# PV of a head group in one run, reciprocals shared by head groups, pruned waits, and scores issued only once ready: a change to a fused adaLN transformer block

## The chip, the cores and the metric

The kernel runs on one core of a Trainium2 chip. The metric is the device time of one execution in microseconds (us); medians of several executions are given. A ratio of two kernels is the mean time of one kernel's fast runs over that of the other's fast runs of the same rounds, so it is not quite the ratio of the medians that stand beside it.

Short names: PE is TensorE's matmuls, PEld its weight loads, ACT ScalarE, DVE VectorE, POOL GpSimd, SP the queue that issues DMAs. L712 is line 712 of the kernel in question, so the same statement has different line numbers before and after (scores: L712 before, L700 after).

## The reference, cut to what matters

```python
# S = 2048 tokens, D = 1024, 32 heads of 32, ONE key/value head, F = 3584; bf16 in and out
mod = silu(c) @ w_mod                      # six vectors: sa, ca, ga, sb, cb, gb
h = layernorm(x) * (1 + ca) + sa
q = (h @ wq) as 32 heads;  k = h @ wk;  v = h @ wv
p = softmax(q @ k.T / sqrt(32));  o = p @ v
x = x + ga * (o @ wo)
h = layernorm(x) * (1 + cb) + sb
x = x + gb * ((silu(h @ w1) * (h @ w3)) @ w2)
```

## The kernel before

The queries are cut into 8 blocks of 256. In a block, 8 *head groups* of 4 heads follow one another, and in a head group 8 *steps* of 2 key tiles. A step is 8 score matmuls (S: 32 rows of the array each, four side by side), then two exps of 128x1024 from PSUM into one of the U buffers. PV matmuls (V: 32 columns each, four side by side) read U. VectorE adds the U buffers of four steps into a TR buffer, and matmuls with a matrix of ones (D) sum TR over the keys, which gives the softmax denominators. After a block's attention come the output projection, layernorm, transposes and the feed-forward of that block ("post"). These use the full array (F) and are slotted into the attention of the next block.

Nothing of this is ordered by hand. Each operation is a node with an assumed duration, and a list scheduler in the kernel fixes the order of every engine when the kernel is built. The parts that the change touches:

```python
slack = 0.12 if e in ("pe", "act") else 0.02      # us
...                                               # scores have the first rank on PE
pick = min((c for c in cands if c[0] <= t + (slack if c[1].prio <= 1 else 0.001)), key=key)
```

`t` is the earliest time at which any candidate can start on the engine. Scores that can start at most 0.12 us later than `t` win against feed-forward work that could start at `t`: PE is parked for them.

```python
NU = 10; VB = 8; R = 8; NTR = 5     # U buffers; key tiles per PV run; TR buffers
...
if len(pend) < vb:                  # vb = 4 steps = 8 key tiles
    continue
g = batch(pend, qn)                 # a PV run into a PSUM bank of its own; reads the key "ATTD"
...                                 # first run: copy the bank to ASB; second run: add it to ASB
for h in range(qn // 128):          # per head group: 2 reciprocals of 128x128
    G.add("dve", lambda e, h=h: e.reciprocal(DSB[:, ...], DSB[:, ...]), ...)
G.add("dve", ... QT[:, f] = ASB * DSB, writes=qkeys(f, q0, qn) + ["ATTD"], ...)
```

Of the eight PSUM banks, six hold scores during attention. The other two are shared by PV/D and by all feed-forward work. Key "ATTD" makes the next head group's PV wait for the normalised output of this one.

The softmax here doesn't subtract the row's maximum and nothing guards it: scores larger than these inputs give would overflow.

Of the kernel before, what the change touches and what calls it, by code (L numbers as in the profile page):

```python
# [3 lines left out]
BF16 = mybir.dt.bfloat16  # L4
F32 = mybir.dt.float32
# [3 lines left out]
P = 128  # L9
# [4 lines left out]
class Node:  # L14
    __slots__ = ("eng", "fn", "dur", "lat", "deps", "prio", "seq", "mode", "acq", "touch",
                 "start", "vis", "pos", "ndeps", "users", "need_inc", "cnt", "dsem", "dval", "nbytes", "est", "cls",
                 "sbanks", "after")
# [8 lines left out]
class Dag:  # L26
# [76 lines left out]
    def schedule(self, banks):  # L103
# [41 lines left out]
        while left:  # L145
# [30 lines left out]
            slack = 0.12 if e in ("pe", "act") else 0.02  # L176
# [70 lines left out]
    def emit(self, tail):  # L247
# [3 lines left out]
        for e in ENGS:  # L251
            seen = {}
            dseen = {}
            for n in self.order[e]:
                need = {}
                dneed = {}
                for d in n.deps:
                    if d.dsem is not None:
                        k = id(d.dsem)
                        if dseen.get(k, 0) < d.dval and (k not in dneed or dneed[k].dval < d.dval):  # L260
                            dneed[k] = d
                    elif d.eng == e == "pe":
                        continue
                    elif seen.get(d.eng, -1) < d.pos and (d.eng not in need or need[d.eng].pos < d.pos):
                        need[d.eng] = d
                for k, d in need.items():
                    seen[k] = d.pos
                    d.need_inc = True
                for k, d in dneed.items():
                    dseen[k] = d.dval  # L270
                waits[id(n)] = (list(need.values()), list(dneed.values()))
# [55 lines left out]
def build(nc, x_in, wq_in, wk_in, wv_in, wo_in, w1_in, w3_in, w2_in, c_in, wmod_in, out, S, D, F):  # L327
# [11 lines left out]
    NU = 10  # L339
    VB = 8  # L340
    R = 8
    NTR = 5
# [20 lines left out]
    ASB = sb("ASB", [P, QB], F32)  # L363
    DSB = sb("DSB", [P, QB], F32)
    WKR = sb("WKR", [P, NC, 4, 32], BF16)
    SCT = sb("SCT", [P, NC], BF16)
# [5 lines left out]
    ONES = sb("ONES", [P, 32], BF16)  # L372
# [36 lines left out]
    def grp():  # L409
        return Group()  # L410


    G.add("pool", lambda e: e.memset(ONES[:], 1.0), writes=["ONES"], dur=0.1)
# [247 lines left out]
    def vmms(e, g, part, last, npk, qn):  # L661
        for n, (pu, pk) in part:
            for j, kt in enumerate(pk):
                for gg in range(4):
                    r = e.matmul(PB[g.bank][32 * gg:32 * gg + 32, 0:qn], V[:, kt, :],  # L665
                                 U[:, pu, (gg * npk + j) * qn:(gg * npk + j + 1) * qn], start=n == 0 and j == 0,
                                 stop=n == last and j == len(pk) - 1, tile_position=(0, 32 * gg),
                                 skip_group_check=True)
        return r

    def batch(pend, qn):

        g = grp()
        last = len(pend) - 1
        npk = 512 // qn
        for w0 in range(0, len(pend), 2):
            part = tuple(enumerate(pend))[w0:w0 + 2]
            dep = pend if w0 == 0 else pend[w0:w0 + 2]
            G.add("pe", lambda e, part=part: vmms(e, g, part, last, npk, qn),
                  reads=sorted({("V", kt // 4) for _, pk in dep for kt in pk}) + ["ATTD"] +  # L680
                  [k for pu, _ in dep for k in (("U", pu, 0), ("U", pu, 1), ("UR", pu))],
                  dur=len(pend[w0:w0 + 2]) * (npk * qn / 2400 + 0.007), lat=0.2, cls="V", mode="V",
                  acq=g if w0 == 0 else None, groups=[(g, "w")])
        return g

    def attention(q0, qn):
# [4 lines left out]
        per_t = ns // (R // npk)  # L691
        per_t = R // npk
        vb = VB // npk
        for f in range(NC):
            pend = []
            trs = []
            for s in range(ns):
# [46 lines left out]
                if len(pend) < vb:  # L744
                    continue
                g = batch(pend, qn)
                pend = []
                if s < ns - 1:
                    if s == vb - 1:
                        G.add("dve", lambda e, g=g: e.tensor_copy(ASB[:, 0:qn], PB[g.bank][:, 0:qn]),  # L750
                              writes=["ASB"], groups=[(g, "r")], dur=dve_t(qn), prio=1)
                    else:
                        G.add("dve", lambda e, g=g: e.tensor_tensor(ASB[:, 0:qn], ASB[:, 0:qn], PB[g.bank][:, 0:qn],
                                                                    ALU.add),
                              reads=["ASB"], writes=["ASB"], groups=[(g, "r")], dur=dve_t(qn), prio=1)
                    continue

                def dmm(e, g=g, trs=tuple(trs)):
                    nn = len(trs) * npk
                    for x in range(nn):  # L760
                        tr, j = trs[x // npk], x % npk
                        for gg in range(4):
                            r = e.matmul(PB[g.bank][32 * gg:32 * gg + 32, qn:2 * qn], ONES[:],  # L763
                                         TR[:, tr, (gg * npk + j) * qn:(gg * npk + j + 1) * qn], start=False,
                                         stop=x == nn - 1, tile_position=(0, 32 * gg), skip_group_check=True)
                    return r
# [183 lines left out]
```

## Time and profile before

| | before |
|---|---|
| time, median | 1261.6 us (1261.06 to 1262.0) |
| PE, DVE, ACT busy | 92%, 82%, 80% of the span |
| last exp ends at | 1066 us |
| streaming of all matmuls at 2.4 GHz | 958 us |

The page of the kernel before, engines (busy us, share of the span, instructions), the granted clock of TensorE in tenths over 40 slices, and the chain that ended last:

```profile
PE 1161.1 (92%) x15762; PEld 760.2 (60%) x15809; DVE 1026.9 (82%) x1475; ACT 1011.3 (80%) x1146; POOL 32.0 (3%) x51
...
PEclk9897999999999999998999899998999989999999
...
ACT 46%; PE 31%; issue 10%; DVE 9%; DMA 3%; SPq 1%; POOL 1%; DVEq 0%; ACTq 0%
```

The chain names ACT first. That is misleading here, and the windows view of the same kernel shows why. Its columns are the stretch, its length, then busy time (and instructions) of PE, PEld, DVE, ACT, POOL, then granted clock, DMA share, GB/s:

```profile
900.00:1000.00 100.00, 97.19 (x1394) 61.87 (x1398) 85.63 (x115) 100.00 (x114) 1.68 (x2) 1.00 0.62 175
1000.00:1100.00 100.00, 94.47 (x1251) 71.53 (x1245) 74.58 (x111) 62.32 (x72) 0.79 (x2) 0.97 0.64 176
1100.00:1180.00 80.00, 78.80 (x700) 67.63 (x700) 40.50 (x68) 8.81 (x14) 1.58 (x4) 1.00 1.05 282
1180.00:1259.00 79.00, 74.18 (x680) 66.25 (x677) 34.57 (x52) 8.81 (x14) 0.00 (x0) 1.00 0.97 246
```

ACT is full until 1000 us and almost idle in the last 159 us, in which PE goes on at 94% and more. That is feed-forward work for which PE found no time earlier. Every us that PE wins during attention shortens this tail.

The waits view of the kernel before (engine, line, releaser: us in all, times, longest), and three lines of its groups of VectorE instructions (busy us, mean ns, idle before):

```profile
PEld SP L712 <- ACT UREG L722: 166.5, 453, 1.7
PE SP L712 <- ACT UREG L722: 26.5, 46, 1.4
```

```profile
L774 DVE RECIPROCAL DSB<-DSB 128x128 f32<-128x128 f32 x128 | 119.4, 939 | 0.4
L750 DVE COPY ASB<-PB 128x256 f32<-128x256 f32 x64 | 26.7, 418 | 6.1 <-PE PB L665 6.0
L769 DVE TENSOR_TENSOR ASB<-ASB,PB 128x256 f32<-128x256 f32 x63 | 26.2, 416 | 25.4 <-PE PB L763 25.1
```

Weight loads before scores wait for ScalarE 453 times, 0.37 us on average. The timeline of PE before, in mid-attention (start, us, operation, count), shows the rhythm: scores (L712) every 1.8 us, feed-forward (L869) between, one of the two PV runs (L665) and the denominators (L763):

```profile
645.14 1.48 PE L869 MATMUL PB<-WREG,HREG 128*128 128x256 bf16 x12
646.56 0.40 PE L712 MATMUL SP<-QT,KT 32*128 32x256 bf16 x8
646.89 0.83 PE L869 MATMUL PB<-WREG,HREG 128*128 128x256 bf16 x6
647.64 1.06 PE L665 MATMUL PB<-UREG,V 128*32 128x256 bf16 x32
648.63 0.40 PE L712 MATMUL SP<-QT,KT 32*128 32x256 bf16 x8
648.96 0.62 PE L763 MATMUL PB<-UREG,ONES 128*32 128x256 bf16 x16
649.51 0.94 PE L869 MATMUL PB<-WREG,HREG 128*128 128x256 bf16 x7
```

Busy time of PE hides gaps here, because a matmul's modelled end lies after the start of the next one (645.14 + 1.48 us is later than 646.56). The Trainium skill also warns that matmul busy time is no good measure of how close a kernel is to the peak ("Perfetto Trace Analysis", Identifying the Most-Contended Engine); the account below agrees, with some 950 us of streaming in 1161 us of busy time. So I also sum **start times**: the gap between two successive matmuls (or sets of four side by side) is the difference of their starts, less columns / 2.4 GHz. Six F matmuls of 256 columns start at 646.89 and take 6 x 0.107 = 0.64 us; PV starts at 647.64, so 0.11 us went into the change. The smallest usual gap is 0.096 to 0.108 us for a change of array shape (F to S 0.098, S to F 0.102, V to S or F 0.108). Within one kind it is 0.003 us (F), 0.013 us (S) and 0.005 us (V, D). I call these floors and everything above them a *stall*.

### The profile page before, as it was taken

Reading aid. Unit: us, or ns where it says so; the run is one execution under the profiler, and the core shown is the slowest. Engines: PE = TensorE matmul, PEld = TensorE weight load, DVE = VectorE, ACT = ScalarE, POOL = GpSimd, SP = SyncE. Lnnn points to the kernel's source line nnn. Section 1 sums busy time; section 2 is a strip of 40 time slices with the busy share of each in tenths; the row PEclk is TensorE's granted clock in tenths of the full one; section 3 lists DMA queues with packets and bytes.
Section 4 is the critical chain, followed back from the end, with each engine's and each line's share of the span. In section 5 each row is a group of like instructions: output and inputs, shape, how many; then the busy total and the mean of one; then the engine's idle time right before and its main releaser. Section 6 shows DMA issues by size and latency. Waiting matters only on the chain.

```text
span 1258.6 us, 36037 instructions
## 1 busy us (share of the span) xinstructions
PE 1161.1 (92%) x15762; PEld 760.2 (60%) x15809; DVE 1026.9 (82%) x1475; ACT 1011.3 (80%) x1146; POOL 32.0 (3%) x51
## 2 busy tenths in 40 slices
PE   4589998999999989998999899998999899999998
PEld 3334333666566646654666466655666567878887
DVE  7888888998989998899988998789988899365352
ACT  1499999999999999999999989998999998011010
POOL 1000001000100000001000100000000000000000
PEclk9897999999999999998999899998999989999999
DMA  9624005755376426851567165654556545999996
GB/s 307 216 82 138 2 2 138 202 153 147 103 218 186 123 65 184 235 152 38 158 192 218 44 169 148 182 151 118 144 159 193 163 134 153 269 295 262 298 292 175
DMA packets 370556, 207.97 MB, mean 165 GB/s; under 512 B 8928, under 2 KB 362208, under 8 KB 370400
## 3 DMA queue, kind: packets, MB, share of 16 engines
q1 hardware_dynamic: 370400, 205.68, 58.1%
q8 instruction: 124, 2.03, 0.7%
q14 instruction: 32, 0.26, 0.1%
HBM read 201.46 MB, written 4.19 MB: 163 GB/s over the span
## 4 chain that ended last, share of the span: by engine, by line
ACT 46%; PE 31%; issue 10%; DVE 9%; DMA 3%; SPq 1%; POOL 1%; DVEq 0%; ACTq 0%
ACT UREG L722 43%; PE PB L835 8%; PE SP L835 6%; PE SP L869 4%; PE PB L869 4%; PE SP L712 3%; DVE UREG L741 2%; PE PB L665 2%; ACT GSB L844 2%; ACT WREG L844 1%; PE PB L812 1%; DMA WREG<-in_w_mod_dram 1%; PE PB L566 1%; DVE UREG L736 1%; DMA UREG<-in_w_mod_dram 1%
## 5 line engine op out<-in xcount | busy, mean ns | idle before, releaser
L722 ACT ACTIVATE UREG<-SP 128x1024 bf16<-128x1024 f32 x1024 | 966.7, 1202 | 39.9 <-PE SP L712 28.0
L741 DVE TENSOR_TENSOR UREG<-UREG 128x2048 bf16<-128x2048 bf16 x256 | 309.7, 1210 | 20.5 <-ACT UREG L722 19.5
L712 PE MATMUL SP<-QT,KT 32*128 32x256 bf16 x4096 | 207.4, 277 | 39.2 <-ACT UREG L722 26.5
L736 DVE TENSOR_TENSOR UREG<-UREG 128x2048 bf16<-128x2048 bf16 x128 | 155.6, 1215 | 45.4 <-ACT UREG L722 44.3
L835 PE MATMUL PB<-QT,WREG 128*128 128x256 bf16 x1440 | 182.1, 275 | 1.7 <-DVE GSB L842 0.6
L712 PEld LDWEIGHTS SP<-QT,KT 32*128 32x128 bf16 x4096 | 61.1, 92 | 185.5 <-ACT UREG L722 166.5
L835 PEld LDWEIGHTS PB<-QT,WREG 128*128 128x128 bf16 x1440 | 131.8, 98 | 41.6 <-issue 27.1
L665 PE MATMUL PB<-UREG,V 128*32 128x256 bf16 x4064 | 140.9, 279 | 9.7 <-DVE HREG L847 3.0
L835 PE MATMUL PB<-QT,HREG 128*128 128x256 bf16 x944 | 124.3, 277 | 1.0 <-DVE QT L527 0.5
L665 PEld LDWEIGHTS PB<-UREG,V 128*32 128x32 bf16 x4064 | 96.3, 97 | 45.5 <-issue 20.0
L844 ACT ACTIVATE GSB<-GSB 128x512 bf16<-128x512 bf16 x56 | 43.2, 771 | 96.4 <-DVE GSB L842 96.4
L774 DVE RECIPROCAL DSB<-DSB 128x128 f32<-128x128 f32 x128 | 119.4, 939 | 0.4
L835 PEld LDWEIGHTS PB<-QT,HREG 128*128 128x128 bf16 x944 | 87.1, 99 | 30.6 <-issue 18.5
L869 PE MATMUL PB<-WREG,HREG 128*128 128x256 bf16 x728 | 91.7, 273 | 0.3 <-DVE DSB L771 0.2
L844 ACT ACTIVATE WREG<-WREG 128x512 bf16<-128x512 bf16 x56 | 42.4, 758 | 55.6 <-DVE WREG L842 55.6
L869 PEld LDWEIGHTS PB<-WREG,HREG 128*128 128x128 bf16 x728 | 66.4, 98 | 20.1 <-issue 13.1
L566 PE MATMUL PB<-HREG,WREG 128*128 128x512 bf16 x238 | 61.1, 380 | 4.5 <-issue 2.5
L835 PE MATMUL PB<-QT,X 128*128 128x256 bf16 x448 | 62.4, 285 | 1.4 <-DVE QT L527 0.9
L812 PE MATMUL PB<-WO,QT 128*128 128x512 bf16 x219 | 57.2, 380 | 4.6 <-DVE QT L569 1.2
L869 PE MATMUL PB<-HREG 128*128 128x256 bf16 x420 | 54.2, 273 | 0.6 <-DVE WREG L875 0.6
L835 PEld LDWEIGHTS PB<-QT,X 128*128 128x128 bf16 x448 | 42.2, 101 | 17.6 <-issue 11.6
L769 DVE TENSOR_TENSOR ASB<-ASB,PB 128x256 f32<-128x256 f32 x63 | 26.2, 416 | 25.4 <-PE PB L763 25.1
(106 smaller groups left out, 1076.7 us busy)
## 6 DMA issues: line engine op xcount, KB each, us to landing
WREG<-in_B_w_dram SPq DMA_DIRECT2D x112, 512.0 KB, 5.0
HREG<-in_B_w_dram SPq DMA_DIRECT2D x74, 512.0 KB, 5.0
WREG<-in_B_w_dram SPq DMA_DIRECT2D x33, 896.0 KB, 5.3
X<-in_B_w_dram SPq DMA_DIRECT2D x38, 512.0 KB, 4.9
HREG<-in_B_w_dram SPq DMA_DIRECT2D x21, 896.0 KB, 5.0
X<-in_B_w_dram SPq DMA_DIRECT2D x10, 896.0 KB, 5.1
X<-in_A_x_dram SPq DMA_DIRECT2D x32, 256.0 KB, 4.8
WREG<-in_w_mod_dram SPq DMA_DIRECT2D x16, 512.0 KB, 4.8
```

The source lines that it names most:

```text
L566: g = mm_group(NC, lambda e, b, c: e.matmul(b, WQ[:, c, f * P:(f + 1) * P], HT[:, c, sl], start=c == 0, stop=c == NC - 1), lambda c: [("WQ ...
L665: r = e.matmul(PB[g.bank][32 * gg:32 * gg + 32, 0:qn], V[:, kt, :], U[:, pu, (gg * npk + j) * qn:(gg * npk + j + 1) * qn], start=n == 0 an ...
L712: r = e.matmul(SP[:, b, o:o + qn], KT[32 * gg:32 * gg + 32, kts[j] * P:(kts[j] + 1) * P], QT[32 * gg:32 * gg + 32, f, q0:q0 + qn], start=T ...
L722: G.add("act", lambda e, u=u, h0=h0, n=n, b0=b0, nb=nb: e.activation(U[:, u, h0 * W:(h0 + n) * W].rearrange("p (b w) -> p b w", b=nb), SP[ ...
L736: G.add("dve", lambda e, tr=tr, u=u, fu=first_u: e.tensor_tensor(TR[:, tr, 0:4 * W], U[:, fu, 0:4 * W], U[:, u, 0:4 * W], ALU.add), reads= ...
L741: G.add("dve", lambda e, tr=tr, u=u: e.tensor_tensor(TR[:, tr, 0:4 * W], TR[:, tr, 0:4 * W], U[:, u, 0:4 * W], ALU.add), reads=[("TR", tr) ...
L769: G.add("dve", lambda e, g=g: e.tensor_tensor(ASB[:, 0:qn], ASB[:, 0:qn], PB[g.bank][:, 0:qn], ALU.add), reads=["ASB"], writes=["ASB"], gr ...
L774: G.add("dve", lambda e, h=h: e.reciprocal(DSB[:, h * 128:(h + 1) * 128], DSB[:, h * 128:(h + 1) * 128]), reads=["DSB"], writes=[("DSBr", ...
L812: g = mm_group(NC, lambda e, b, f, t=t, h=h: e.matmul(b, QT[:, f, t * P:(t + 1) * P], WO[:, f, h * 512:(h + 1) * 512], start=f == 0, stop= ...
L835: return e.matmul(b[:, j * qn:(j + 1) * qn], w13[:, w, c, j * P:(j + 1) * P], QT[:, c, q0:q0 + qn], start=c == 0, stop=c == NC - 1)
L844: G.add("act", lambda e, b=b: e.activation(TB[b], GS[b], ACT.Tanh, scale=0.5), reads=[("GS", b)], writes=[("TB", b)], clear=alias("TB") if ...
L869: G.add("pe", lambda e, g=g, j=j, fc=fc, hf=hf, first=first, w2s=w2s: e.matmul(PB[g.bank][:, j * 256:(j + 1) * 256], HHT[:, hf * NH + fc, ...
```

## The change

Its intent: give VectorE less to do, hand PSUM over once per head group instead of twice, send fewer semaphore waits, and never park PE for scores. The diff, cut to its core:

```diff
-            slack = 0.12 if e in ("pe", "act") else 0.02
+            slack = {"pe": 0.0, "act": 0.12}.get(e, 0.02)
 ...  (emit: a wait is left out when another wait of the same engine already implies it)
-    NU = 10
-    VB = 8
-    R = 8
-    NTR = 5
+    NU = 11
+    NTR = 4
+    DGRP = ((0, 1, 2, 3), (4, 5, 6), (7,))
 ...
-    ONES = sb("ONES", [P, 32], BF16)
+    SEL = sb("SEL", [P, len(DGRP), 4, 32], BF16)      # ones in the columns of member j, zeros elsewhere
 ...  (PV: one PSUM group over all 8 steps, in pieces of 2 steps; one copy to ASB[f % 4]; key "ATTD" is gone)
+            if gj == 0:    DSB[da] = bank        # first member of a group of head groups
+            else:          DSB[da] += bank       # the others fill other rows of the same tile
+            if not last:   continue
+            for h in range(qn // 128):           # 2 reciprocals per group of 4, 3 or 1 head groups
+                ... e.reciprocal(DSB[:, da, ...], DSB[:, da, ...])
+            for ff in DGRP[ga]:
+                ... e.stream_shuffle(RB, DSB[:, da], [cut] * 32)   # this member's row to its 32 rows
+                ... QT[:, ff] = ASB[:, ff % 4] * RB
```

More of the change, by code (lines that the diff above doesn't have):

```diff
@@ L16 @@
                  "start", "vis", "pos", "ndeps", "users", "need_inc", "cnt", "dsem", "dval", "nbytes", "est", "cls",
-                 "sbanks", "after")
+                 "sbanks", "after", "know")
 class Group:
@@ L250, in emit @@
         waits = {}
-        for e in ENGS:
-            seen = {}
-            dseen = {}
-            for n in self.order[e]:
-                need = {}
-                dneed = {}
-                for d in n.deps:
-                    if d.dsem is not None:
-                        k = id(d.dsem)
-                        if dseen.get(k, 0) < d.dval and (k not in dneed or dneed[k].dval < d.dval):
-                            dneed[k] = d
-                    elif d.eng == e == "pe":
+        cur = {e: ({}, {}) for e in ENGS}
+        for n in sorted(self.nodes, key=lambda n: (n.start, n.pos)):
+            e = n.eng
+            ck, cd = cur[e]
+            need, dneed = [], []
+            for d in sorted(n.deps, key=lambda d: (-d.vis, -d.start, -d.pos)):
+                if d.dsem is not None:
+                    if cd.get(id(d.dsem), 0) >= d.dval:
                         continue
-                    elif seen.get(d.eng, -1) < d.pos and (d.eng not in need or need[d.eng].pos < d.pos):
-                        need[d.eng] = d
-                for k, d in need.items():
-                    seen[k] = d.pos
+                    dneed.append(d)
+                else:
+                    if d.eng == e == "pe" or ck.get(d.eng, -1) >= d.pos:
+                        continue
                     d.need_inc = True
-                for k, d in dneed.items():
-                    dseen[k] = d.dval
-                waits[id(n)] = (list(need.values()), list(dneed.values()))
+                    need.append(d)
+                dk, dd = d.know
+                for k, v in dk.items():
+                    if ck.get(k, -1) < v:
+                        ck[k] = v
+                for k, v in dd.items():
+                    if cd.get(k, 0) < v:
+                        cd[k] = v
+            waits[id(n)] = (need, dneed)
+            nk, nd = dict(ck), dict(cd)
+            if n.dsem is not None:
+                nd[id(n.dsem)] = max(nd.get(id(n.dsem), 0), n.dval)
+            elif nk.get(e, -1) < n.pos:
+                nk[e] = n.pos
+            n.know = (nk, nd)
         for e in ENGS:
@@ L362, in build @@
     XN = sb("XN", [P, 4, D], BF16)
-    ASB = sb("ASB", [P, QB], F32)
-    DSB = sb("DSB", [P, QB], F32)
+    RB = sb("RB", [P, QB], F32)
     WKR = sb("WKR", [P, NC, 4, 32], BF16)
+    ASB = XN[:, 2:4, :].rearrange("p a d -> p (a d)").bitcast(F32).rearrange("p (a q) -> p a q", a=4)
+    DSB = WKR[:].rearrange("p c a f -> p (c a f)").bitcast(F32).rearrange("p (a q) -> p a q", a=2)
     SCT = sb("SCT", [P, NC], BF16)
@@ L410, in grp @@
         return Group()
-    G.add("pool", lambda e: e.memset(ONES[:], 1.0), writes=["ONES"], dur=0.1)
+    cuts = {}
+    G.add("pool", lambda e: e.memset(SEL[:], 0.0), writes=["SEL"], dur=0.3)
+    for a, fs in enumerate(DGRP):
+        edge = [32 * j // len(fs) for j in range(len(fs) + 1)]
+        for j, f in enumerate(fs):
+            cuts[f] = (a, j, edge[j])
+            G.add("pool", lambda e, a=a, j=j, edge=edge: e.memset(SEL[:, a, j, edge[j]:edge[j + 1]], 1.0),
+                  reads=["SEL"], writes=["SEL"], dur=0.1)
     G.add("pool", lambda e: e.memset(NHALF[:], -0.5), writes=["NHALF"], dur=0.1)
@@ L659, in build @@
     tr_count = [0]
-    def vmms(e, g, part, last, npk, qn):
-        for n, (pu, pk) in part:
-            for j, kt in enumerate(pk):
-                for gg in range(4):
-                    r = e.matmul(PB[g.bank][32 * gg:32 * gg + 32, 0:qn], V[:, kt, :],
-                                 U[:, pu, (gg * npk + j) * qn:(gg * npk + j + 1) * qn], start=n == 0 and j == 0,
-                                 stop=n == last and j == len(pk) - 1, tile_position=(0, 32 * gg),
-                                 skip_group_check=True)
-        return r
-    def batch(pend, qn):
-        g = grp()
-        last = len(pend) - 1
-        npk = 512 // qn
-        for w0 in range(0, len(pend), 2):
-            part = tuple(enumerate(pend))[w0:w0 + 2]
-            dep = pend if w0 == 0 else pend[w0:w0 + 2]
-            G.add("pe", lambda e, part=part: vmms(e, g, part, last, npk, qn),
-                  reads=sorted({("V", kt // 4) for _, pk in dep for kt in pk}) + ["ATTD"] +
-                  [k for pu, _ in dep for k in (("U", pu, 0), ("U", pu, 1), ("UR", pu))],
-                  dur=len(pend[w0:w0 + 2]) * (npk * qn / 2400 + 0.007), lat=0.2, cls="V", mode="V",
-                  acq=g if w0 == 0 else None, groups=[(g, "w")])
-        return g
     def attention(q0, qn):
@@ L690, in attention @@
         ns = NT // npk
-        per_t = ns // (R // npk)
-        per_t = R // npk
-        vb = VB // npk
+        per_t = 8 // npk
         for f in range(NC):
@@ L743, in attention @@
                         reads=[("TR", tr)] + ur, writes=[("TR", tr)], dur=dve_t(4 * npk * qn, 2), prio=3)
-                if len(pend) < vb:
-                    continue
-                g = batch(pend, qn)
-                pend = []
-                if s < ns - 1:
-                    if s == vb - 1:
-                        G.add("dve", lambda e, g=g: e.tensor_copy(ASB[:, 0:qn], PB[g.bank][:, 0:qn]),
-                              writes=["ASB"], groups=[(g, "r")], dur=dve_t(qn), prio=1)
-                    else:
-                        G.add("dve", lambda e, g=g: e.tensor_tensor(ASB[:, 0:qn], ASB[:, 0:qn], PB[g.bank][:, 0:qn],
-                                                                    ALU.add),
-                              reads=["ASB"], writes=["ASB"], groups=[(g, "r")], dur=dve_t(qn), prio=1)
-                    continue
@@ L758, in dmm @@
-                def dmm(e, g=g, trs=tuple(trs)):
-                    nn = len(trs) * npk
-                    for x in range(nn):
-                        tr, j = trs[x // npk], x % npk
-                        for gg in range(4):
-                            r = e.matmul(PB[g.bank][32 * gg:32 * gg + 32, qn:2 * qn], ONES[:],
-                                         TR[:, tr, (gg * npk + j) * qn:(gg * npk + j + 1) * qn], start=False,
-                                         stop=x == nn - 1, tile_position=(0, 32 * gg), skip_group_check=True)
-                    return r
@@ L767, in attention @@
-                G.add("pe", dmm, reads=["ONES"] + [("TR", tr) for tr in trs] + [("UR", NU + tr) for tr in trs],
-                      dur=len(trs) * npk * (qn / 2400 + 0.0035), lat=0.2, groups=[(g, "w")], mode="V", cls="D")
-                G.add("dve", lambda e, g=g: e.tensor_tensor(ASB[:, 0:qn], ASB[:, 0:qn], PB[g.bank][:, 0:qn], ALU.add),
-                      reads=["ASB"], writes=["ASB"], groups=[(g, "r")], dur=dve_t(qn), prio=1)
-                G.add("dve", lambda e, g=g: e.tensor_copy(DSB[:, 0:qn], PB[g.bank][:, qn:2 * qn]), writes=["DSB"],
-                      groups=[(g, "r")], dur=dve_t(qn), prio=1)
@@ L773, in attention @@
-            for h in range(qn // 128):
-                G.add("dve", lambda e, h=h: e.reciprocal(DSB[:, h * 128:(h + 1) * 128], DSB[:, h * 128:(h + 1) * 128]),
-                      reads=["DSB"], writes=[("DSBr", h), "DSB%d" % h], dur=0.87, prio=2 if f == NC - 1 else 4)
-            G.add("dve", lambda e, f=f: e.tensor_tensor(QT[:, f, q0:q0 + qn], ASB[:, 0:qn], DSB[:, 0:qn], ALU.mult),
-                  reads=["ASB", "DSB"] + [("DSBr", h) for h in range(qn // 128)], writes=qkeys(f, q0, qn) + ["ATTD"],
-                  dur=dve_t(qn), prio=2 if f == NC - 1 else 4)
+            g = grp()
@@ new lines, in attention, with vmm @@
+            for w0 in range(0, ns, 2):
+                part = pend[w0:w0 + 2]
+                def vmm(e, g=g, part=tuple(part), w0=w0):
+                    for n, (pu, pk) in enumerate(part):
+                        for j, kt in enumerate(pk):
+                            for gg in range(4):
+                                r = e.matmul(PB[g.bank][32 * gg:32 * gg + 32, 0:qn], V[:, kt, :],
+                                             U[:, pu, (gg * npk + j) * qn:(gg * npk + j + 1) * qn],
+                                             start=w0 + n == 0 and j == 0, stop=w0 + n == ns - 1 and j == len(pk) - 1,
+                                             tile_position=(0, 32 * gg), skip_group_check=True)
+                    return r
+                dep = pend if w0 == 0 else part
+                G.add("pe", vmm, reads=sorted({("V", kt // 4) for _, pk in dep for kt in pk}) +
+                      [k for pu, _ in dep for k in (("U", pu, 0), ("U", pu, 1), ("UR", pu))],
+                      dur=len(part) * (npk * qn / 2400 + 0.007), lat=0.2, cls="V", mode="V",
+                      acq=g if w0 == 0 else None, groups=[(g, "w")])
@@ new lines, in attention, with dmm @@
+            ga, gj, cut = cuts[f]
+            last = gj == len(DGRP[ga]) - 1
+            da = ga % 2
+            pr = 2 if f == NC - 1 else 4
+            def dmm(e, g=g, trs=tuple(trs), ga=ga, gj=gj):
+                nn = len(trs) * npk
+                for x in range(nn):
+                    tr, j = trs[x // npk], x % npk
+                    for gg in range(4):
+                        r = e.matmul(PB[g.bank][32 * gg:32 * gg + 32, qn:2 * qn], SEL[:, ga, gj, :],
+                                     TR[:, tr, (gg * npk + j) * qn:(gg * npk + j + 1) * qn], start=False,
+                                     stop=x == nn - 1, tile_position=(0, 32 * gg), skip_group_check=True)
+                return r
@@ new lines, in attention @@
+            G.add("pe", dmm, reads=["SEL"] + [("TR", tr) for tr in trs] + [("UR", NU + tr) for tr in trs],
+                  dur=len(trs) * npk * (qn / 2400 + 0.0035), lat=0.2, groups=[(g, "w")], mode="V", cls="D")
+            G.add("dve", lambda e, g=g, f=f: e.tensor_copy(ASB[:, f % 4, 0:qn], PB[g.bank][:, 0:qn]),
+                  writes=[("ASB", f % 4), ("XN", 2 + f % 4 // 2)], groups=[(g, "r")], dur=dve_t(qn), prio=1)
+            if gj == 0:
+                G.add("dve", lambda e, g=g, da=da: e.tensor_copy(DSB[:, da, 0:qn], PB[g.bank][:, qn:2 * qn]),
+                      writes=[("DSB", da), "WKR"], groups=[(g, "r")], dur=dve_t(qn), prio=1)
+            else:
+                G.add("dve", lambda e, g=g, da=da: e.tensor_tensor(
+                    DSB[:, da, 0:qn], DSB[:, da, 0:qn], PB[g.bank][:, qn:2 * qn], ALU.add),
+                    reads=[("DSB", da)], writes=[("DSB", da)], groups=[(g, "r")], dur=dve_t(qn), prio=1)
@@ new lines, in attention @@
+            if not last:
+                continue
+            for h in range(qn // 128):
+                G.add("dve", lambda e, h=h, da=da: e.reciprocal(DSB[:, da, h * 128:(h + 1) * 128],
+                                                                DSB[:, da, h * 128:(h + 1) * 128]),
+                      reads=[("DSB", da)], writes=[("DSBr", da, h)], dur=0.87, prio=pr)
+            rk = [("DSB", da)] + [("DSBr", da, h) for h in range(qn // 128)]
+            for ff in DGRP[ga]:
+                if len(DGRP[ga]) > 1:
+                    G.add("dve", lambda e, da=da, c=cuts[ff][2]: e.stream_shuffle(
+                        RB[:, 0:qn], DSB[:, da, 0:qn], [c] * 32), reads=rk, writes=["RB"], dur=dve_t(qn) + 0.06, prio=pr)
+                    rb, kk = RB[:, 0:qn], ["RB"]
+                else:
+                    rb, kk = DSB[:, da, 0:qn], rk
+                G.add("dve", lambda e, ff=ff, rb=rb: e.tensor_tensor(
+                    QT[:, ff, q0:q0 + qn], ASB[:, ff % 4, 0:qn], rb, ALU.mult), reads=[("ASB", ff % 4)] + kk,
+                    writes=qkeys(ff, q0, qn), dur=dve_t(qn), prio=pr)
```

## The prediction

> **What bounds the kernel.** TensorE's instruction stream. The page shows PE 92% busy, DVE 82%, ACT 80%, but ACT's share mixes two stages. In the windows view ACT is 93 to 100% busy from 120 to 1000 us (attention; its last exp ends at 1066 us) and then almost idle, while PE goes on at about 98% with 185 us of feed-forward left over. PE fits that work into attention wherever it has time, so each microsecond of PE freed there shortens the tail. ACT's pace does not set the end: only the last block's part of the tail, about 85 us (estimate), must follow attention.
>
> The Trainium skill ("Perfetto Trace Analysis", Identifying the Most-Contended Engine) warns that matmul busy time is no measure of headroom. This trace agrees: by PE's matmul start times, streaming at 2.4 GHz takes only 947 of 1259 us. The rest: about 1160 changes of tile shape of at least 0.10 us (118 us; "TensorEngine Tiling", Key Properties, says a mode change drains TensorE); about 36 us of issue gaps; 40 us of start-up; about 100 us of stalls. The largest stall stands before scores: feed-forward to scores costs 0.21 us mean (median 0.18) where 0.10 is the floor, x427, thus about 45 us. The waits view agrees: the weight loads of L712 wait for ACT 453 times, 166 us, of which 0.21 us each is only the drain.
>
> **What the change does.**
> 1. Scores only once ready: the scheduler no longer parks PE for up to 0.12 us before scores; it puts another 0.109 us matmul there. ACT starts 0.05 to 0.13 us after its scores end (floor 0.05), so ACT has some 0.08 us to spare and may lose a little, off the end. I expect 25 to 30 us of PE stall gone.
> 2. PV in one run: one PSUM hand-over and about one shape change less per head group, 64 x 0.10 = 6 us of PE; ASB's second add goes (64 x 0.416 = 27 us of DVE).
> 3. Shared reciprocals: 128 x 0.939 = 120 us falls to 48 x 0.94 = 45 us; 56 shuffles of 128x256 cost about 0.42 us each (estimate from the equal f32 copies), +24 us. DVE falls from 1027 to about 950 us. It is not the bound; earlier evictions and sums save perhaps 5 us of PE stalls.
> 4. Pruned waits: about 1 us.
> Scores, PV and denominators stream the same columns as before.
>
> **Sum.** 28 + 6 + 5 + 1 = 40 us: 1222 us, -3.1%. Range 1200 to 1247. Chances: faster 0.75, within 2% 0.22, slower 0.03.
>
> **What would show it.** Step 1: median gap to scores 0.10 to 0.12 us, PE idle before L712 from 39 to about 15 us; the last exp at about the same time, the tail some 40 us shorter. Step 2: fewer PV stretches. Step 3: reciprocal x48, DVE below 960 us. PE streaming stays at 947 us.
>
> **What would make it wrong.** The stall before scores may come from ACT being slower than the schedule's model (then PE still stalls; gain 10 to 15 us). The PV run over 16 tiles holds one of two PSUM banks for over 2 us and may starve the feed-forward, or its 0.44 us pieces may delay scores until ACT stalls and PE runs out of filler in the first block. A lower granted clock at denser PE work would give some back. If reclaimed stalls are larger than I count, 1200 is possible.

## The result, and the profile after

The changed kernel takes 1218.28 us (median of 4 runs, 1216.69 to 1218.84) against 1261.8 us (4 runs, 1261.06 to 1263.31). The ratio is 0.9656, 95% interval 0.9643 to 0.967. The predicted time was 1222 us.

The page after, the same three lines:

```profile
PE 1137.2 (93%) x15809; PEld 767.5 (63%) x15809; DVE 967.1 (79%) x1443; ACT 1019.8 (84%) x1146; POOL 29.6 (2%) x59
...
PEclk9797998999989999999999998999999999999999
...
PE 72%; ACT 19%; DVE 5%; DMA 2%; issue 1%; SPq 1%; POOL 0%
```

PE now stands where ACT stood in the chain. The windows after:

```profile
900.00:1000.00 100.00, 95.57 (x1461) 63.64 (x1460) 88.54 (x131) 99.40 (x114) 2.53 (x4) 1.00 0.58 164
1000.00:1100.00 100.00, 99.69 (x1326) 73.00 (x1327) 80.68 (x125) 75.15 (x86) 1.95 (x4) 1.00 0.72 203
1100.00:1180.00 80.00, 80.00 (x736) 71.70 (x734) 39.14 (x62) 9.63 (x16) 0.00 (x0) 1.00 1.10 286
1180.00:1219.00 39.00, 32.24 (x296) 28.66 (x293) 9.99 (x16) 1.70 (x3) 0.00 (x0) 0.95 0.72 180
```

The last exp ends at 1072 us, 6 us later than before, and the tail behind it is 145 us instead of 193 us. More matmuls fit into the same time: 1461 instead of 1394 between 900 and 1000 us. The waits and two groups after:

```profile
PEld SP L700 <- ACT UREG L710: 86.7, 224, 1.7
...
PEld SP L700 <- issue: 56.4, 258, 0.8
...
PE SP L700 <- ACT UREG L710: 23.5, 32, 1.4
```

```profile
L779 DVE RECIPROCAL WKR<-WKR 128x128 f32<-128x128 f32 x48 | 44.5, 938 | 0.2
...
L785 DVE STREAM_SHUFFLE RB<-WKR 128x256 f32<-128x256 f32 x56 | 24.6, 440 | 0.0
```

Half of the waits of score weight loads for ScalarE are now "issue": the scores are ready when PE comes to them, and 0.22 us (56.4 / 258) is how long the weight loads' track then stands idle at a change of shape. The timeline of PE after, around a PV run (L741; L761 are the denominators):

```profile
458.13 1.06 PE L741 MATMUL PB<-UREG,V 128*32 128x256 bf16 x32
459.12 0.40 PE L700 MATMUL SP<-QT,KT 32*128 32x256 bf16 x8
459.45 1.06 PE L741 MATMUL PB<-UREG,V 128*32 128x256 bf16 x32
460.33 0.61 PE L761 MATMUL PB<-UREG,SEL 128*32 128x256 bf16 x16
```

PV is still cut once by scores, but PV and denominators now follow each other without a change of shape.

The account of PE's time by start times, which the rest of this text uses (us, after the first 80 us unless said; one profiled run of each kernel):

| | before | after |
|---|---|---|
| streaming, small gaps, start and end (same in both) | 958 + 28 + 9 | 958 + 28 + 10 |
| changes of shape: number, time | 1166, 118 | 1080, 109 |
| stalls before scores that follow F (median gap) | 38.9 (0.185) | 6.2 (0.098) |
| stalls between two sets of scores | 7.9 | 15.1 |
| other stalls at full clock | 36.3 | 27.5 |
| lost while TensorE ran at half clock (whole span) | 29 | 33 |
| start-up stalls, first 80 us | 34 | 30 |
| sum | 1259 | 1217 |

The stall before scores gives 33 of the 42 us, changes of shape and other stalls 9 each, start-up 4; stalls between scores and the half clock take 11 back. (The trace of before lacks the records of 47 matmuls: the page has PE x15762 against PEld x15809, and the lacking ones are all of 512 columns. I put them back from the weight loads. In the prediction they were not put back, so its 947 us of streaming was 10 us too low and its stalls as much too high. The pages of a_recip1_dve84, a_pv2_guard, a_dve74 and a_act2 lack 39 to 47 records in the same way.)

An account says where time was, not what a part of the change is worth. For that the parts have to be taken apart.

### The profile page after: what moved, and what is told of

Same layout as the page of the kernel before. It is cut to its first block, busy times and chain, and to the rows that moved or that the text cites. A ratio compares the mean times of both kernels' runs of the same rounds, so it can differ in the third digit from the quotient of the medians.

```text
span 1217.0 us, 35301 instructions
## 1 busy us (share of the span) xinstructions
PE 1137.2 (93%) x15809; PEld 767.5 (63%) x15809; DVE 967.1 (79%) x1443; ACT 1019.8 (84%) x1146; POOL 29.6 (2%) x59
## 4 chain that ended last, share of the span: by engine, by line
PE 72%; ACT 19%; DVE 5%; DMA 2%; issue 1%; SPq 1%; POOL 0%
PE PB L849 24%; ACT UREG L710 18%; PE PB L883 11%; PE SP L700 10%; PE PB L741 8%; PE SP L849 5%; PE PB L581 4%; PE SP L883 4%; PE PB L826 2%; PE PB L761 2%; DVE UREG L724 1%; DMA WREG<-in_w_mod_dram 1%; DMA UREG<-in_w_mod_dram 1%; DVE ST L492 1%; DVE HREG L542 1%
## 5 line engine op out<-in xcount | busy, mean ns | idle before, releaser
L729 DVE TENSOR_TENSOR UREG<-UREG 128x2048 bf16<-128x2048 bf16 x256 | 311.6, 1217 | 25.3 <-ACT UREG L710 23.6
L700 PE MATMUL SP<-QT,KT 32*128 32x256 bf16 x4096 | 207.5, 278 | 30.0 <-ACT UREG L710 23.5
L724 DVE TENSOR_TENSOR UREG<-UREG 128x2048 bf16<-128x2048 bf16 x128 | 156.5, 1223 | 84.3 <-ACT UREG L710 83.6
L849 PE MATMUL PB<-QT,WREG 128*128 128x256 bf16 x1552 | 193.6, 273 | 2.3 <-DVE GSB L856 0.7
L849 PEld LDWEIGHTS PB<-QT,WREG 128*128 128x128 bf16 x1552 | 142.3, 98 | 43.8 <-issue 28.3
L741 PE MATMUL PB<-UREG,V 128*32 128x256 bf16 x4096 | 133.7, 279 | 4.4 <-DVE GSB L856 2.0
L849 PE MATMUL PB<-QT,HREG 128*128 128x256 bf16 x1024 | 131.0, 275 | 1.6 <-DVE WREG L856 0.7
L741 PEld LDWEIGHTS PB<-UREG,V 128*32 128x32 bf16 x4096 | 102.4, 98 | 29.5 <-issue 15.8
L849 PEld LDWEIGHTS PB<-QT,HREG 128*128 128x128 bf16 x1024 | 94.4, 98 | 30.4 <-issue 19.2
L858 ACT ACTIVATE GSB<-GSB 128x512 bf16<-128x512 bf16 x56 | 37.3, 666 | 61.1 <-DVE GSB L856 61.1
L883 PE MATMUL PB<-WREG,HREG 128*128 128x256 bf16 x672 | 86.5, 273 | 0.3 <-DVE WREG L889 0.3
L883 PEld LDWEIGHTS PB<-WREG,HREG 128*128 128x128 bf16 x672 | 61.2, 98 | 20.6 <-issue 12.9
L883 PE MATMUL PB<-HREG 128*128 128x256 bf16 x448 | 59.6, 277 | 1.4 <-DVE WREG L889 1.1
L849 PE MATMUL PB<-QT,X 128*128 128x256 bf16 x448 | 56.8, 273 | 0.8 <-DVE WREG L856 0.5
L883 PEld LDWEIGHTS PB<-HREG 128*128 128x128 bf16 x448 | 41.2, 99 | 16.3 <-issue 10.6
L779 DVE RECIPROCAL WKR<-WKR 128x128 f32<-128x128 f32 x48 | 44.5, 938 | 0.2
```

What stands on the lines that cost most here:

```text
L700: r = e.matmul(SP[:, b, o:o + qn], KT[32 * gg:32 * gg + 32, kts[j] * P:(kts[j] + 1) * P], QT[32 * gg:32 * gg + 32, f, q0:q0 + qn], start=T ...
L724: G.add("dve", lambda e, tr=tr, u=u, fu=first_u: e.tensor_tensor(TR[:, tr, 0:4 * W], U[:, fu, 0:4 * W], U[:, u, 0:4 * W], ALU.add), reads= ...
L729: G.add("dve", lambda e, tr=tr, u=u: e.tensor_tensor(TR[:, tr, 0:4 * W], TR[:, tr, 0:4 * W], U[:, u, 0:4 * W], ALU.add), reads=[("TR", tr) ...
L741: r = e.matmul(PB[g.bank][32 * gg:32 * gg + 32, 0:qn], V[:, kt, :], U[:, pu, (gg * npk + j) * qn:(gg * npk + j + 1) * qn], start=w0 + n == ...
L779: G.add("dve", lambda e, h=h, da=da: e.reciprocal(DSB[:, da, h * 128:(h + 1) * 128], DSB[:, da, h * 128:(h + 1) * 128]), reads=[("DSB", da ...
L849: return e.matmul(b[:, j * qn:(j + 1) * qn], w13[:, w, c, j * P:(j + 1) * P], QT[:, c, q0:q0 + qn], start=c == 0, stop=c == NC - 1)
```

## The experiments

Theory P, from the prediction: PE's instruction stream sets the end; most of the gain is PE no longer parked before scores; one PV run and less VectorE work are small extras. Rival D: it is the relief of VectorE. Rival W: it is the fewer waits. Rival B: it is the PSUM hand-over. Later came rival L: an edit merely draws another instruction order, lucky or unlucky. Ratios are to the kernel before, run on the same chip in the same rounds; every run was correct.

### Undoing one part of the change

**a_slack12**: PE may be parked again.

```diff
-            slack = {"pe": 0.0, "act": 0.12}.get(e, 0.02)
+            slack = 0.12 if e in ("pe", "act") else 0.02
```

> The changed kernel with the scheduler's old rule back: TensorE may again be parked up to 0.12 us for scores that are not ready. Theory P (most of the gain is parked TensorE time before scores): 1240 to 1250 us, feed-forward to scores gap back to a median of about 0.18 us. Rival D (gain is VectorE relief) and rival W (gain is fewer waits): 1218 to 1224 us.

Measured 1256.16 us (ratio 0.9963, 0.9937 to 0.9988), 38 us above the changed kernel. The median gap from F to S went back to 0.185 us and the stall there to 43 us. The waits view of this kernel is that of before:

```profile
PEld SP L700 <- ACT UREG L710: 171.7, 480, 1.9
```

Attention got *shorter* (last exp at 1041 us instead of 1072) and the kernel slower. This is theory P's picture, with a cost above its range (1240 to 1250 us expected).

**a_recip1**: own reciprocals for each head group, no shuffles.

```diff
-    DGRP = ((0, 1, 2, 3), (4, 5, 6), (7,))
+    DGRP = tuple((f,) for f in range(8))
```

> The changed kernel with one reciprocal pair per head group again and no shuffles (48 reciprocals become 128, 56 shuffles go; VectorE about +50 us busy). Theory P: VectorE is off the path, 1218 to 1224 us. Rival D: 1232 us or more.

Measured 1246.69 us (0.9885, 0.987 to 0.99): 28 us slower, though VectorE has only 37 us more to do (1004.6 against 967.1 us) and is 81% busy. Theory P said 1218 to 1224 us; here it failed, and rival D's number was met. The account shows stalls between scores up from 15 to 24 us, other stalls from 28 to 34 us, and the half-clock loss from 33 to 44 us.

**a_pv2**: PV in two runs of 8 key tiles, with the second add into ASB.

```diff
+                if s % (ns // 2) < ns // 2 - 1:
+                    continue
+                r0 = s - ns // 2 + 1          # a run, a bank and an evict of its own per 4 steps
+                ... ASB copy for r0 == 0, ASB add for the second run
```

> The changed kernel with PV of a head group in two runs of 8 key tiles and a second add into ASB; 11 U buffers stay. Theory P with one shape change per head group: 1223 to 1229 us. If the PSUM hand-over mattered more (rival B, bank held less often): 1235 us or more. Rivals D and W: within 4 us of 1218 us.

Measured 1262.23 us (1.0004, 0.9987 to 1.0021): 44 us slower. Theory P's number (1223 to 1229 us) failed and rival B's (1235 us or more) was met. The changes of shape account for 11 us of it (1186 instead of 1080), which is what theory P had. The rest is 15 us more stall before scores (with the median gap still 0.098 us, so the added stall is in a few longer waits), 18 us more other stall and 7 us more half-clock loss, less 9 us between scores.

**a_oldwaits**: the old, unpruned waits.

```diff
-        cur = {e: ({}, {}) for e in ENGS}     # ... waits implied by others left out
+        for e in ENGS:                        # ... one wait per engine and DMA, as before
```

> The changed kernel with the old, unpruned waits and the same instruction order on every engine. Theory P: 1218 to 1221 us. Rival W (redundant waits cost issue time on TensorE or ScalarE): 1230 us or more.

Measured 1220.46 us (0.968, 0.9661 to 0.9699, against 0.9656, 0.9643 to 0.967): 2 us, and the intervals overlap. Rival W is out.

Three parts undone one at a time cost 38, 28 and 44 us, 110 us in all, where the whole change gained 43.5 us. So the parts are not terms of a sum.

### Adding parts to the kernel before

**b_slack0**: only the rule for scores. **b_pv16**: only PV in one run. **b_pv16_slack0**: both.

```diff
# b_slack0
-            slack = 0.12 if e in ("pe", "act") else 0.02
+            slack = {"pe": 0.0, "act": 0.12}.get(e, 0.02)
# b_pv16
-    NU = 10; VB = 8; NTR = 5
+    NU = 11; VB = 16; NTR = 4
-                ... tensor_tensor(ASB, ASB, PB[g.bank], ALU.add)
+                ... tensor_copy(ASB, PB[g.bank])
```

> The kernel before with the one rule of scores only once ready. Theory P (parked TensorE is the whole story): 1225 to 1232 us. Theory I (rule and one PV run only pay together, because work to fill the gap needs a free PSUM bank): 1238 to 1250 us, gain 12 to 24 of the 43 us. Rival L (the order of the tuned schedule was lucky, any edit loses it): 1262 us or more.

> The kernel before with PV over 16 key tiles in one run (11 U buffers, 4 TR buffers), nothing else. Theory I: within 8 us of before (1254 to 1270 us), as parked TensorE does not use the freed PSUM time. Rival B (PSUM hand-over by itself sets the time): 1235 us or less.

> Both together on the kernel before, each head group still with its own reciprocals and old waits. Theory I: 1230 to 1245 us, more gain than the two alone add up to. Theory P: no better than b_slack0. Rival L: 1255 us or more.

Measured: b_slack0 1238.04 us (0.9816, 0.9798 to 0.9835), b_pv16 1276.41 us (1.0117, 1.0098 to 1.0135), both 1249.58 us (0.9902, 0.9886 to 0.9919). Misses: theory P for b_slack0 (1225 to 1232 us), theory I for b_pv16 (1254 to 1270 us) and for both together (1230 to 1245 us), and rival B for b_pv16 (1235 us or less).

- The rule for scores gains 24 us on the kernel before, 27 us on b_pv16 and 38 us on the rest of the change: three pairs, one sign. Of the two parts tried alone it is the one that pays by itself; shared reciprocals alone were not tried.
- PV in one run *costs* 14 us by itself and 12 us with the rule, although it saves 84 to 113 changes of shape in either pair. Theory I, that rule and run pay only together, is wrong: the two together give 12 us, about the sum of -24 and +14.
- With one run, sharing the reciprocals seems to turn the cost into a gain: from b_pv16_slack0 (1249.6 us) or a_recip1 (1246.7 us, nearly the same kernel) to the changed kernel is another 28 to 31 us. How much of that is only the order drawn is tested below.

### Why one run: how long PV holds a PSUM bank

**a_pv2h**: a_pv2, but both runs add up in one bank that is held from the first run to the last: no second hand-over and no second add.

```diff
-                g = grp()
+                if r0 == 0:
+                    g = grp()
-                if r0 == 0:   (copy of the first half to ASB)
```

> The changed kernel with PV in two runs of 8 key tiles that keep one PSUM bank from the first run to the last: no second hand-over and no second add, but the bank is held some 10 us per head group instead of 4 us (estimate from the program's order). Theory bank time (one run helps because PV holds a PSUM bank for less time): 1270 us or more, worse than a_pv2 at 1262 us. Theory count (one run helps by fewer hand-overs, adds and shape changes): 1225 to 1255 us, better than a_pv2.

Measured 1295.46 us (1.0263, 1.0245 to 1.0281), as theory bank time said: 33 us slower than a_pv2, though it has less VectorE work (975.3 against 989.0 us busy). In this pair a longer hold of the bank cost more than one hand-over and one add saved. From the trace, the time in which some PV group holds a bank, from its first matmul to the end of the last VectorE read of its bank, in the whole kernel:

| | PV holds a bank | time |
|---|---|---|
| a_pv2h | 631 us | 1295 us |
| a_pv2 | 343 us | 1262 us |
| changed kernel | 254 us | 1218 us |

Two banks serve all feed-forward work of the attention stage, so a bank that PV holds is a stretch in which only one feed-forward group can be open. That a much longer hold costs time is what the pair shows. That a shorter one gains is not shown: b_pv16 holds 304 us against 342 us before and is 14 us slower, b_pv16_slack0 264 us against 345 us in b_slack0 and is 12 us slower, and a_recip1 holds 260 us and takes 1247 us.

**a_pv2_guard**: a_pv2 with the key "ATTD" of the kernel before put back.

```diff
+ ... reads of a PV run:  + ["ATTD"]
+ ... writes of QT:       + ["ATTD"]
```

> a_pv2 with the ordering key ATTD of the kernel before put back (a PV run waits until the last normalised group has been written). It tells how much of a_pv2's 44 us belongs to PV in two runs and how much to the guard that the change dropped along with them. If two runs alone cost it: 1255 us or more. If the missing guard let PV take a PSUM bank too early: 1236 to 1250 us.

Measured 1255.95 us (0.9948, 0.9931 to 0.9965). Putting the guard back gives 6 of a_pv2's 44 us in this order. The time meets "1255 us or more" by 1 us. Two PV runs with shared reciprocals are thus 18 us slower than two PV runs with own ones (b_slack0; the two kernels differ in buffers and waits too), while with one run sharing gains about 30 us.

### Is it only the order that the scheduler happens to draw?

**a_recip1_dve84** and **a_dve74**: the same work as a_recip1 and the changed kernel, with another assumed VectorE overhead in the scheduler. That alters only what the scheduler draws: the order of instructions and which bank a group gets.

```diff
-    return n / rate / 960.0 + 0.08
+    return n / rate / 960.0 + 0.084     # a_recip1_dve84;  0.074 in a_dve74
```

> a_recip1 (own reciprocals) with the schedule's assumed VectorE overhead at 0.084 instead of 0.080 us: the same work, another instruction order. If a_recip1's 1247 us was an unlucky order: 1218 to 1228 us. If own reciprocals cost time at block borders, where TensorE idles and its clock is halved: 1235 us or more, with at least 80 us at half clock again (after: 65 us, a_recip1: 93 us).

> The changed kernel with the schedule's assumed VectorE overhead at 0.074 instead of 0.080 us: the same work, another order, one in which TensorE is left less idle. Scatter of the order alone is about 5 us (estimate), so 1213 to 1223 us if it is only scatter; 1200 to 1210 us if the order chosen is better on the chip too, which would beat both kernels.

Measured: a_recip1_dve84 1233.52 us (0.9774, 0.9759 to 0.9789), 13 us better than a_recip1 by order alone, and 15 us slower than the changed kernel. It falls short of the "1235 us or more" that I had set for a cost of the reciprocals, and is far from "1218 to 1228 us": half of a_recip1's 28 us was the draw. (The other half of that expectation was met: the clock record gives 91 us at half clock, 80 us or more expected.) a_dve74 takes 1200.77 us (0.9512, 0.9498 to 0.9526), 17.5 us better than the changed kernel with the same work. It beats both kernels, and the 5 us of scatter that I had estimated was far too little. So rival L is partly right: **two orders of the same work differ by 13 to 17 us**, and a difference of that size between two kernels of different order cannot be put down to the work. These are two pairs only, so 17 us is no upper limit of what an order can do. Above it lie the rule for scores in the pair with the changed kernel (38 us; the other two pairs, 24 and 27 us, too), one run with shared reciprocals (38 to 44 us), and a_pv2h against a_pv2 (33 us). The plus of 12 to 14 us for one run alone, the 18 us of sharing with two runs, and the last 15 us of own reciprocals do not. For shared reciprocals with one run it speaks that both orders with them (1218 and 1201 us) beat both with own ones (1247 and 1234 us).

### What goes wrong at the block borders

The granted clock gave the lead. The cores view (span, mean granted clock) of the changed kernel, of a_recip1 and of a_dve74, in this order:

```profile
core 0: 1217.0 us, clock 0.974
```

```profile
core 0: 1245.6 us, clock 0.963
```

```profile
core 0: 1196.8 us, clock 0.983
```

The clock records are 1 or 0.5, so 2 x (1 - 0.963) x 1245.6 = 92 us of a_recip1 ran at half clock, against 63 us and 41 us. After the first 120 us and before the end there are 8 such spells in a_recip1, 7 in a_recip1_dve84, 5 in the changed kernel, 3 in a_dve74. Each is 3.4 to 10.2 us long, and most come some 130 us apart, at the border of two blocks. The Trainium skill ("TensorE: Matmul & The Clock Gate", What's actually happening) describes the two clock states and says that the clock halves after an idle window; the halving shows in this trace, a wholly idle window does not (last section). The timeline of PE of a_recip1 at one border:

```profile
473.29 0.40 PE L527 MATMUL PB<-IDENT,XN 128*128 128x128 bf16 x4
474.17 0.40 PE L527 MATMUL PB<-IDENT,XN 128*128 128x128 bf16 x4 [0.48 <-DVE WREG L889]
474.50 0.40 PE L700 MATMUL SP<-QT,KT 32*128 32x256 bf16 x8
476.13 0.40 PE L700 MATMUL SP<-QT,KT 32*128 32x256 bf16 x8 [1.23 <-ACT UREG L710]
477.96 0.40 PE L700 MATMUL SP<-QT,KT 32*128 32x256 bf16 x8 [1.44 <-ACT UREG L710]
479.40 1.04 PE L527 MATMUL PB<-IDENT,XN 128*128 128x128 bf16 x8 [1.04 <-DVE XN L513]
480.37 0.61 PE L700 MATMUL SP<-QT,KT 32*128 32x256 bf16 x8
481.80 3.56 PE L741 MATMUL PB<-UREG,V 128*32 128x256 bf16 x64 [0.83 <-DVE QT L542]
...
486.06 1.16 PE L883 MATMUL PB<-HREG 128*128 128x256 bf16 x9
```

From 474.5 to 479.4 us PE runs nothing but scores. The finished block's transposes (L527) come in two groups with a PSUM bank each, and each group needs the layernorm (XN, L513) of two token tiles. Their first halves, at 473.29 and 474.17 us, have taken both banks, and XN of the second tile comes only at 478.79 us. Until then no other group has a bank, although feed-forward of the block before (L883, from 486.06 us) is left. The 64 PV matmuls that follow take 3.56 us, about twice their 1.7 us (64 / 4 x 0.107), because the clock has been halved at 478 us. VectorE in the same stretch:

```profile
467.08 0.94 DVE L779 RECIPROCAL WKR<-WKR 128x128 f32<-128x128 f32 x1
...
469.02 0.67 DVE L829 TENSOR_TENSOR X<-X,PB 128x512 bf16<-128x512 bf16 x1
469.62 0.94 DVE L779 RECIPROCAL WKR<-WKR 128x128 f32<-128x128 f32 x1
470.58 0.42 DVE L790 TENSOR_TENSOR QT<-XN,WKR 128x256 bf16<-128x256 f32 x1
...
478.79 0.55 DVE L513 TENSOR_SCALAR XN<-X,MV,RS 128x1024 bf16<-128x1024 bf16 x1 [0.77 <-POOL RS L501]
```

The reciprocals and the product of the *next* block's first head group stand, 2.3 us in all, among the residual adds of the finished block (L829), ahead of its layernorm. In the changed kernel there are none at the matching border (462 to 476 us): the first head group's reciprocals wait for those of the fourth, when the border is over. PE finds feed-forward matmuls between all scores there, and no half-clock spell occurs. So VectorE matters where its queue is a chain that PE waits for, though on average it is idle for a fifth of the time. That the 2.3 us are what tips this border is read from one pair of timelines; no run isolated it.

They are not needed for it. At an earlier border of the changed kernel the transposes take both banks too, with no reciprocal on VectorE from 325 to 345 us:

```profile
338.62 0.40 PE L527 MATMUL PB<-IDENT,XN 128*128 128x128 bf16 x4 [0.46 <-DVE WREG L889]
339.22 0.40 PE L527 MATMUL PB<-IDENT,XN 128*128 128x128 bf16 x4 [0.20 <-DVE X L829]
...
344.44 1.03 PE L527 MATMUL PB<-IDENT,XN 128*128 128x128 bf16 x8 [0.67 <-DVE XN L513]
```

The clock is halved at 341.2 us, for 10.2 us. A count over all 14 traces finds 52 such holes: at least 3.4 us with no matmul but scores while the transposes are half done. A half-clock spell followed every one. There are 7 holes each in a_recip1 and b_pv16_slack0 and 6 in a_recip1_dve84, but 3 in the changed kernel and 2 in a_dve74. So with one run and the new rule for scores, own reciprocals go with more of these holes. No run changed the transposes alone, so what a hole costs is not shown by an experiment.

### What sets the end

**a_act2**: every second head group does one exp twice.

```diff
+                    if s == 3 and h == 1 and f % 2:
+                        G.add("act", ... the same activation(U[...], SP[...], ACT.Exp, scale=SCALE) again)
```

> The changed kernel with one exp in every second head group done twice (32 more, about 0.90 us each, 29 us more ScalarE work, same result). Theory P (TensorE's stream sets the end, not ScalarE): last exp 20 us or more later, time within 8 us of 1218 us. Rival A (ScalarE sets the end, as the chain of waits before had 46% ScalarE): 1240 to 1250 us.

Measured 1221.23 us (0.967; the changed kernel had 0.9656): 3 us for 30 us more ScalarE work (1050.1 us busy against 1019.8), in the one order that was run. The last exp ends at 1112 us, 40 us later. Its windows view, columns as above:

```profile
1000.00:1100.00 100.00, 96.95 (x1439) 67.33 (x1430) 83.08 (x121) 98.62 (x113) 2.39 (x3) 1.00 0.65 186
1100.00:1180.00 80.00, 79.55 (x784) 66.46 (x779) 51.12 (x88) 18.19 (x25) 1.58 (x4) 1.00 0.91 242
```

Attention reaches further into the tail and the tail shrinks by as much. ScalarE does not set the end, although it is 93% to 100% busy for 800 us and led the chain before.

All accounts on one page, without a_oldwaits, which has the changed kernel's order (us, one profiled run each; "scores" is the stall from F to S, "between" from S to S):

| kernel | time | changes | half clock | scores | between | other |
|---|---|---|---|---|---|---|
| before | 1261.8 | 118 | 29 | 38.9 | 7.9 | 36.3 |
| b_slack0 | 1238.0 | 118 | 24 | 12.7 | 9.5 | 42.7 |
| b_pv16 | 1276.4 | 109 | 43 | 38.5 | 12.4 | 43.8 |
| b_pv16_slack0 | 1249.6 | 107 | 50 | 8.5 | 24.8 | 31.5 |
| a_recip1 | 1246.7 | 107 | 44 | 8.8 | 23.5 | 34.0 |
| a_recip1_dve84 | 1233.5 | 107 | 50 | 6.1 | 19.9 | 24.1 |
| a_pv2h | 1295.5 | 121 | 34 | 43.9 | 9.0 | 56.6 |
| a_pv2 | 1262.2 | 120 | 40 | 21.6 | 6.0 | 45.2 |
| a_pv2_guard | 1256.0 | 117 | 44 | 9.2 | 18.3 | 39.9 |
| a_slack12 | 1256.2 | 110 | 24 | 43.1 | 2.9 | 45.8 |
| changed kernel | 1218.3 | 109 | 33 | 6.2 | 15.1 | 27.5 |
| a_act2 | 1221.2 | 110 | 43 | 6.2 | 14.0 | 30.4 |
| a_dve74 | 1200.8 | 110 | 22 | 3.5 | 10.5 | 26.1 |

Read it by columns. The rule for scores nearly empties "scores" in every pair that differs in it alone. One PV run takes 9 to 13 us from "changes". In the kernels with one run and own reciprocals, that saving is lost again under "half clock" and, with the rule, under "between". The changed kernel and a_dve74 are low in nearly all columns.

## Why the prediction was right or wrong, point by point

The time was right: 1222 us predicted, 1218.3 us measured. Not all of its terms were.

- **PE's stream sets the end.** Right. 30 us more of ScalarE work cost 3 us (a_act2).
- **Streaming 947 us, stalls about 100 us.** Off by 10 us, because 47 matmul records are lacking in the trace of before; 958 us is right.
- **Step 1, 25 to 30 us of stall before scores.** Right in mechanism and nearly in size. The stall fell by 33 us in the account, the median gap from 0.185 to 0.098 us (predicted 0.10 to 0.12); alone the rule gains 24 us, and taking it away costs 38 us. PE idle before the scores fell from 39.2 to 30.0 us only, not to 15, because stalls between two sets of scores grew by 7 us.
- **Step 2, one PV run saves 6 us.** The changes of shape did fall, by 86 (9 us), but as a term of the sum the step failed. The prediction counted it as a saving that stands by itself: added to the kernel before, it cost 14 us (b_pv16), and taken from the changed kernel it cost 38 to 44 us. What the prediction had listed as a danger, that PV holds one of two PSUM banks, is real where the hold is long: 631 us gave 1295 us (a_pv2h). In the change the hold fell, from 342 to 254 us, but a shorter hold did not gain by itself (b_pv16).
- **Step 3, VectorE is not the bound, perhaps 5 us.** VectorE's work fell by 60 us (to 967.1 us, not below 960 us as predicted; reciprocals from 119.4 to 44.5 us, shuffles 24.6 us as estimated). Its worth was mis-sized: own reciprocals cost 15 to 28 us in two orders. The mean load of 82% said nothing about the block borders, where PE waits for VectorE's chain with both PSUM banks taken, and then loses its clock too.
- **Step 4, pruned waits about 1 us.** Right: 2 us, within the noise.
- **28 + 6 + 5 + 1 = 40 us.** The sum was right in size partly by luck. Its terms are not additive (undone one by one they give 110 us), and the order of the same work alone moves the time by 13 to 17 us, which the prediction had not considered. The range of 47 us covered that.

What stays open: why sharing the reciprocals gains with one PV run and does not with two. The holes at the block borders, with their stalls and half clock, name a place. Part of the contrast (18 us) is no larger than what an order can do, and telling them apart would need several orders of each kernel.

## What to carry to other kernels

Where one engine is full throughout and another only in a stage, ask which of them still has work when the stage ends; the chain of waits may name the wrong one. In a kernel whose order a scheduler draws, run a second order of the same work before you put 15 us down to an edit, and then take the best order: here that gave 17.5 us for a changed constant. And look for an engine with a low mean load at the borders of stages, where its queue is a chain and an idle TensorE pays again in clock. Look there also for half-done groups that hold all free PSUM banks.

## What the Trainium skill lacked or had wrong

- "TensorE: Matmul & The Clock Gate", What's actually happening: it ties the half clock to an idle window of about 3.4 us, without a figure for how idle. In the changed kernel five spells of 3.4 to 10.2 us came after the first 120 us, and in the 8 us before each of them no gap between two matmuls was longer than 1.61 us. I cut all 14 traces into the 3.41 us steps on which the clock records lie, and took the share of each step that matmuls streamed (columns / 2.4 GHz). Between the first 120 us and the last 6 us there are 80 spells. Each followed a step with a share of 6% to 38%. The 4318 steps at full clock that no spell followed had 37% or more. So TensorE need not be wholly idle: in these runs a step with less than about 37% of streaming was enough. The same page's section on psum-queue depth-cycling does say that frequent short idle times can make the clock swing, but gives no figure for how short.
- "TensorEngine Tiling (Array Packing)", Key Properties: it says that a change of mode drains TensorE, without a figure. Here it costs 0.096 to 0.108 us at full clock, and about 1100 changes took 107 to 121 us, 9% of the time.
- "VectorE: DVE Perf Modes", the perf-mode tier table: it has STREAM_SHUFFLE at 2048 elements only. A shuffle of 128x256 f32 took 0.440 us on average, a PSUM-to-SBUF f32 copy of that size 0.42 us.
- No page that I read says that matmul records can be lacking in a trace while weight loads are complete: 15762 against 15809 before. Comparing the two counts shows it.
